# Two sets of weight sums on GpSimd, moved from two turns of the attention loop to its last turn

## The chip, the cores and the metric

The kernel runs on one core of one Trainium2 chip. A core has five engines with instruction streams of their own: TensorE (PE, with its weight loads listed as PEld), VectorE (DVE), ScalarE (ACT), GpSimd (POOL) and SyncE (SP), which here only starts transfers. The metric is the device time of one execution in microseconds (us), as a median over several runs.

## What is computed

An attention block with clusters feeds a two-layer network. Queries and keys are each assigned to the best of 16 centroids of their head; a query attends only to keys of its own cluster. The attention's output, laid out as 3072 tokens by 512 features, goes through the network with the activation h * sigmoid(1.702 h). The reference, cut to that:

```python
# q, k, v: (4 batches, 8 heads, 768, 64); centroids: (8, 16, 64); w_in (512, 2048), w_out (2048, 512)
mask = q_assign[:, :, :, None] == k_assign[:, :, None, :]
scores = np.where(mask, scale * np.matmul(q, k.transpose(0, 1, 3, 2)), -1000000000.0)
attn = np.exp(scores - np.max(scores, axis=-1, keepdims=True))
attn = attn / (np.sum(attn, axis=-1, keepdims=True) + 1e-09)
x = np.matmul(attn, v)                     # then (B,H,S,D) -> (B*S, H*D)
h = x @ w_in
g = h * (1.0 / (1.0 + np.exp(-1.702 * h)))
return g @ w_out
```

The two weight matrices arrive in double precision and are rounded on the chip.

## The kernel before

**Attention.** Heads go in pairs: 4 batches with 4 pairs each make 16 pairs (numbered 0 to 15 in the code, one to sixteen in words). A pair is done in two halves of 384 queries; a half has six units, one for each 128 keys. The main loop runs over turns `t` of two units each, so a half is three turns, a pair six, and all of attention 96 turns (`NT`), with two more to drain. The first turn of pair thirteen is turn 72, and that of pair fourteen is turn 78. The order of every engine's work is the order in which the program issues it; no scheduler moves it (`manual_schedule`). Each engine works through its own queue in order and waits at an instruction until what it needs is there.

In one turn, TensorE makes two units of transposed scores (`scores`, L453) and adds the cluster terms that push other clusters' scores far down (`part`, L476); ACT takes the exponentials into a tile `A` of 128 keys by 2 heads by 384 queries (`exps`, L484); and TensorE multiplies the previous turn's `A` with the values (`values`, L518). The softmax denominators need the sum of a half's six `A` tiles. `add_up` makes it, on GpSimd (L502, one instruction per head), except the first addition of every even half, which is VectorE's (L495), and the last two tiles of the very last half, which go to TensorE as they are (`last`). There are four `A` tiles, so an exponential can start only when GpSimd and TensorE are through with the tile of four units earlier. Once a half is summed, `row_sums_of` (L535) multiplies the sum with a constant tile on TensorE, and `normalise` (L545 to L561) turns, inverts and applies the result on VectorE. For the last batch the normalised tile goes out to memory (`kept`, L561, on SP's queue) and comes back later.

Beside that, each pair's turns prepare the next pair: its turned copies (L308, VectorE), its cluster scores (`prep_near`, L329, TensorE, once in a pair and in its first turn), its assignment and the transfers that spread it. Two of a pair's turns each also round one piece of the weights (five instructions on VectorE, two checks on ACT).

**The network.** It starts when attention ends. Both matrix products are done with seven block products in place of eight: the blocks of one operand are first added and subtracted with one another, and so are the results. For the first product, `w_in` is taken in eight strips (`f`), used for each of the four batches (`b`). For every strip a set of sums of four blocks of `w_in` is made on GpSimd, by `sums_w(i)` with i = 8 b + f. A set has four sums of 128x256 (L589 is the line of the helper that makes all such sums): S3, written in place into `w_in` and made only for the first batch, then S2, S1 and S4 in a tile `W`. There are two `W` tiles, so a set can be begun in a tile only when TensorE is through with the set two before it.

```python
        if i < FB:
            sums(nc.gpsimd, ((S[3], A11, "-", S[3]),))
        sums(nc.gpsimd, ((S[2], A22, "-", S[3]), (S[1], S[2], "+", A11),
                         (S[4], A12, "-", S[2])))
```

`first7(b, f)` makes the seven products of a strip (L743). In their order they use A11 of `w_in` (no sum), S2, S1, S3, S4, and then two more blocks of `w_in` itself. ACT copies the first result into a buffer `G` (L752), and VectorE adds the others to it (L734). After each `first7` the main loop asks for the set two ahead, `sums_w(b * FB + f + 2)`, and, for the first batch, for sums of blocks of `w_out` (`sums_z`). The sets 0 and 1 have no such place: they are made in the attention loop, at turns 72 and 78 (`NT - 24`, `NT - 18`).

Of the kernel before, what the change touches and what calls it, by code (L numbers as in the profile page):

```python
# [18 lines left out]
def kernel(  # L19
    tc: tile.TileContext,  # L20
    q: bass.AP,
    k: bass.AP,
    v: bass.AP,
    centroids: bass.AP,
    moe_w_in: bass.AP,
    moe_w_out: bass.AP,
    out: bass.AP,
):

    args = (q, k, v, centroids, moe_w_in, moe_w_out, out)
    bad = fast(tc, *args)
    with tc.If(bad > 0):
        general(tc, *args)
# [3 lines left out]
def fast(  # L39
# [172 lines left out]
    def step():  # L212

        if not now and w_done[0] < NW:
            now.append(rounding())
        if now:
            n = w_done[0]
            next(now[0])
            if w_done[0] > n:
                now.clear()  # L220
# [225 lines left out]
    def scores(u):  # L446
        g, kt = divmod(u, NJ)
        p, h = split(g)
        ps = ps_s.tile([P, 2, 512], FP32, name="s")
        for a in range(2):  # L450
            rows = slice(a * D, (a + 1) * D)
            for c in range(0, P, D):
                nc.tensor.matmul(  # L453
                    out=ps[c:c + D, a, 0:HALF],
                    lhsT=T[p, 1][rows, kt * P + c:kt * P + c + D],
                    rhs=T[p, 0][rows, h * HALF:(h + 1) * HALF],
                    start=True, stop=False)
        s_of[u] = ps[:, :, 0:HALF]

    def part(u):  # L460

        g, kt = divmod(u, NJ)
        p, h = split(g)
        if p == 0:
            for a in range(2):
                r = SQ * a
                nc.tensor.matmul(
                    out=s_of[u][:, a, :],
                    lhsT=hots[1][r:r + NC, kt * P:(kt + 1) * P],
                    rhs=hots[0][r:r + NC, h * HALF:(h + 1) * HALF],  # L470
                    start=False, stop=True)
            return
        for a in range(2):
            rows = slice(a * D, (a + 1) * D)
            for c in range(0, P, D):
                nc.tensor.matmul(  # L476
                    out=s_of[u][c:c + D, a, :],
                    lhsT=rows_of[1, p % 2][rows, kt * P + c:kt * P + c + D],
                    rhs=rows_of[0, p % 2][rows, h * HALF:(h + 1) * HALF],
                    start=False, stop=True)  # L480

    def exps(u):
        A_of[u] = ap.tile([P, 2, HALF], FP32, name="A")
        nc.scalar.activation(out=A_of[u], in_=s_of.pop(u), func=AF.Exp,  # L484
                             scale=SCALE)

    def add_up(u):

        g, kt = divmod(u, NJ)
        if kt == 0:  # L490
            return
        if kt == 1:
            sum_of[g] = ap.tile([P, 2, HALF], FP32, name="sum", bufs=2)
        if kt == 1 and g % 2 == 0:
            later.append(lambda: nc.vector.tensor_tensor(  # L495
                out=sum_of[g], in0=A_of[u - 1], in1=A_of[u], op=ALU.add))
            return
        if g == NG - 1 and kt >= NJ - 2:
            last.append(A_of[u])
            return  # L500
        for a in range(2):
            nc.gpsimd.tensor_tensor(  # L502
                out=sum_of[g][:, a],
                in0=(A_of[u - 1] if kt == 1 else sum_of[g])[:, a],
                in1=A_of[u][:, a], op=ALU.add)
# [3 lines left out]
    def values(u):  # L509
        g, kt = divmod(u, NJ)  # L510
        p, h = split(g)
        if kt == 0:
            o_of[g] = ps_o.tile([P, 2, 512], FP32, name="o")
        A = A_of.pop(u)
        for r in range(2):
            rows = slice(r * D, (r + 1) * D)
            for a in range(2):
                nc.tensor.matmul(out=o_of[g][a * D:(a + 1) * D, r, 0:HALF],  # L518
                                 lhsT=v_in[p][rows, a, kt, :],
                                 rhs=A[rows, a, :],  # L520
                                 start=(kt == 0), stop=(kt == NJ - 1))
        if kt == NJ - 1:
            o = o_of.pop(g)
            O_of[g] = (xp if p < NPAIR - HP else xl).tile(
                [P, HALF], FP32, name="x"), short()
            for r in range(2):
                nc.scalar.copy(O_of[g][r], o[:, r, 0:HALF])

    def row_sums_of(g):

        ps = ps_of[g] = bank()
        parts = (last if g == NG - 1 else []) + [sum_of.pop(g)]
        for i, sm in enumerate(parts):
            for a in range(2):
                nc.tensor.matmul(out=ps[a * D:(a + 1) * D, 0:HALF], lhsT=twos,  # L535
                                 rhs=sm[:, a, :], start=(i == 0),
                                 stop=(i == len(parts) - 1))
# [28 lines left out]
    def check(g):  # L566


        rec = recs.pop(g)
        nc.scalar.activation(out=rec, in_=rec, func=AF.Copy,  # L570
                             accum_out=row_sums[:, 0, g:g + 1])
        nc.scalar.activation(out=rec, in_=rec, func=AF.Relu, bias=top[:, 0:1],
                             scale=-2.0 * LIMIT * LIMIT,
                             accum_out=row_sums[:, 1, g:g + 1])
# [12 lines left out]
    def sums(engine, todo):  # L587
        for o, a, op, b in todo:
            engine.tensor_tensor(out=o, in0=a, in1=b, op=(  # L589
                ALU.add if op == "+" else ALU.subtract))  # L590
# [3 lines left out]
    def A_in(row, col, f):  # L594

        at = (row * FB + f) * P
        return w_in[:, 2 * col:2 * col + 2, at:at + P]
# [3 lines left out]
    def sums_w(i):  # L601

        if i >= B * FB:
            return
        f = i % FB
        S = wq.tile([P, 3, 2, P], FP32, name="W")
        w_of[i] = {1: S[:, 0], 2: S[:, 1], 3: A_in(1, 0, f), 4: S[:, 2]}
        S = w_of[i]
        A11, A12, A22 = A_in(0, 0, f), A_in(0, 1, f), A_in(1, 1, f)
# [4 lines that stand above are left out]
# [19 lines left out]
    NT = NU // 2  # L633
# [3 lines left out]
    for p in range(1, NPAIR):  # L637
        for i in range(2 if p == 1 else 0, len(PREP)):
            t = 2 * TG * (p - 1) + (0, 0, 0, 0, 1, 2, 2)[i]
# [5 lines left out]
    def prep(p, i):  # L645
        if i == 2 and p:
            load_v(p)
        PREP[i](p)
        if i in (1, 3) and loads:
            load_qk(*loads.popleft())  # L650
# [7 lines left out]
    for t in range(NT + 2):  # L658
        us = range(2 * t, 2 * t + 2) if t < NT else ()
        for u in us:  # L660
            scores(u)
        if t == 0:
            prep(0, 6)
        for u in us:
            part(u)
        for u in us:
            exps(u)
        if recs:
            check(*recs)
        for u in us:  # L670
            add_up(u)
        work = sorted(prep_at.get(t, ()), key=lambda w: PREP[w[1]] != prep_near)
        turns = [w for w in work if w[1] < 4]
        for p, i in turns:
            prep(p, i)
        work = [w for w in work if w[1] >= 4]
        while later:
            later.pop()()
        if 1 <= t <= NT:
            for u in range(2 * t - 2, 2 * t):  # L680
                values(u)
        if t >= 2 and (t - 2) % TG == TG - 1:
            row_sums_of((t - 2) // TG)
        while work and PREP[work[0][1]] == prep_near:
            prep(*work.pop(0))
        if t in (NT - 24, NT - 18):
            sums_w(t // (NT - 18))
        if t >= NT - 8 and t < NT:
            XT = next(made)
        for p, i in work:  # L690
            prep(p, i)
        for _ in range(0 if t in (0, 1, 2, NT - 1) else 5 if t == 4 else
                       steps[t % (2 * TG)]):
            step()
        if t >= 2 and (t - 2) % TG == TG - 1:
            normalise((t - 2) // TG)
# [607 lines left out]
```

## Time and profile before

| | |
|---|---|
| median of 3 runs | 939.36 us (939.26 to 939.95) |
| profiled execution, its time | 939.74 us |
| profiled execution, its span | 937.8 us |
| PE busy | 920.5 us (98% of the span) |
| PEld busy | 578.4 us (62%) |
| VectorE busy | 624.0 us (67%) |
| ACT busy | 326.0 us (35%) |
| GpSimd busy | 420.8 us (45%), of which 266.2 us additions of A tiles at L502 (252, mean 1091 ns) |
| first product of the network (L743) | starts at 352.95 us |
| granted TensorE clock | 0.997 of full speed |

Times inside the profile count from the span's start. A line of the order in time gives the start, the busy time of the run of instructions, engine, line, operation, the tile written and read, the shape, the count, and in brackets how long the engine had been idle and who released it. The share of busy time is a mean over two parts that differ: attention up to 352.95 us, and the network after it, so the prediction reads stretches, not the whole.

### The profile page before, as it was taken

To read this page: it belongs to the slowest core of one execution; us is meant where nothing else is said; L and a number is where in the kernel's file an instruction comes from. 1 tells how busy PE (TensorE), PEld (TensorE's weight loads), DVE (VectorE), ACT (ScalarE), POOL (GpSimd) and SP (SyncE) were. 2 spreads that over 40 slices of the span, in tenths; PEclk is the share of its full clock that TensorE was granted. 3 is DMA by queue.
4 is the path that set the end of the run, shared out by engine and by line. 5 is a ranking of instruction groups with operands and counts; after the bars stand their busy time and mean duration, and the time that the engine had idled before them with its cause. 6 is when DMAs were issued, how large, how long until landed. Compare 5 with 4: busy or idle time off the path is not lost.

```text
span 937.8 us, 16591 instructions
## 1 busy us (share of the span) xinstructions
PE 920.5 (98%) x6469; PEld 578.4 (62%) x6469; DVE 624.0 (67%) x1077; ACT 326.0 (35%) x703; POOL 420.8 (45%) x440
## 2 busy tenths in 40 slices
PE   6999999999999999999999999999999999999997
PEld 2344444444444445558886557887557887556886
DVE  3999999989988896775345775344776343677331
ACT  3667767767776672221001221001222000232000
POOL 5899899899999996772001220001211000120000
PEclk9999999999999999999999999999999999999999
DMA  9465556566543210011000000000000000000000
GB/s 184 101 128 101 99 103 138 106 121 114 103 99 98 81 49 10 0 29 40 23 23 22 1 0 1 23 23 24 0 1 1 23 23 23 0 1 1 23 24 26
DMA packets 138215, 46.65 MB, mean 50 GB/s; under 512 B 127256, under 2 KB 132496, under 8 KB 138128
## 3 DMA queue, kind: packets, MB, share of 16 engines
q1 hardware_dynamic: 137984, 45.48, 22.1%
q8 instruction: 53, 0.87, 0.4%
q14 instruction: 34, 0.28, 0.1%
q10 hardware_dynamic: 144, 0.03, 0.0%
HBM read 37.44 MB, written 8.05 MB: 49 GB/s over the span
## 4 chain that ended last, share of the span: by engine, by line
PE 84%; POOL 4%; DVE 4%; issue 3%; ACT 2%; DMA 1%; SPq 1%; ACTq 0%; DVEq 0%; POOLq 0%
PE b L800 31%; PE b L743 31%; PE s L453 9%; PE o L518 7%; POOL sum L502 4%; PE m L535 2%; PE s L476 2%; ACT A L484 1%; PE m L329 1%; DMA line<-row 0%; DVE x L556 0%; SPq L404 0%; DMA raw<-in_moe_w_out_dram 0%; DVE e L200 0%; PE m L315 0%
## 5 line engine op out<-in xcount | busy, mean ns | idle before, releaser
L502 POOL TENSOR_TENSOR sum<-sum,A 128x384 f32<-128x384 f32 x252 | 266.2, 1091 | 33.6 <-ACT A L484 21.3
L589 POOL TENSOR_TENSOR W<-w_in 128x256 f32<-128x256 f32 x32 | 23.3, 729 | 379.6 <-PE b L743 379.4
L484 ACT ACTIVATE A<-s 128x768 f32<-128x768 f32 x192 | 145.1, 804 | 99.4 <-PE s L476 76.3
L734 DVE TENSOR_TENSOR G<-b,G 128x384 f32<-128x384 f32 x224 | 124.4, 556 | 62.7 <-PE b L743 50.4
L453 PE MATMUL s<-T,T 64*64 64x384 f32 x1536 | 145.8, 494 | 2.7 <-ACT A L484 0.7
L734 DVE TENSOR_TENSOR y<-b,y 128x256 f32<-128x256 f32 x72 | 29.5, 423 | 171.7 <-PE b L800 121.8
L518 PE MATMUL o<-A,inv 64*64 64x384 f32 x1536 | 141.5, 483 | 0.0
L579 ACT ACTIVATE th<-G 128x384 f32<-128x384 f32 x128 | 67.0, 523 | 208.8 <-DVE G L734 128.5
L580 DVE SCALAR_TENSOR_TENSOR G<-th,G 128x384 f32<-128x384 f32 x128 | 91.3, 713 | 23.0 <-ACT th L579 19.1
L453 PEld LDWEIGHTS s<-T,T 64*64 64x64 f32 x1536 | 52.7, 132 | 79.0 <-ACT A L484 51.3
L743 PE MATMUL b<-x,W 128*128 128x384 f32 x256 | 93.0, 486 | 0.0
L743 PE MATMUL b<-T,w_in 128*128 128x384 f32 x256 | 93.0, 486 | 0.0
L743 PE MATMUL b<-x,w_in 128*128 128x384 f32 x256 | 88.5, 486 | 0.0
L800 PE MATMUL b<-Z,G 128*128 128x256 f32 x384 | 86.8, 379 | 0.0
L800 PE MATMUL b<-w_out,G 128*128 128x256 f32 x384 | 84.8, 379 | 0.0
L518 PEld LDWEIGHTS o<-A,inv 64*64 64x64 f32 x1536 | 58.9, 133 | 38.3 <-issue 33.2
L800 PEld LDWEIGHTS b<-w_out,G 128*128 128x128 f32 x384 | 72.8, 190 | 10.9
L800 PEld LDWEIGHTS b<-Z,G 128*128 128x128 f32 x384 | 73.0, 190 | 9.9
L743 PEld LDWEIGHTS b<-x,W 128*128 128x128 f32 x256 | 48.6, 190 | 33.9
L743 PEld LDWEIGHTS b<-T,w_in 128*128 128x128 f32 x256 | 48.6, 190 | 33.9
L743 PEld LDWEIGHTS b<-x,w_in 128*128 128x128 f32 x256 | 48.6, 190 | 33.6 <-issue 0.6
L810 ACT COPY y<-b 128x256 f32<-128x256 f32 x12 | 4.5, 372 | 141.5 <-PE b L800 141.5
(120 smaller groups left out, 1130.6 us busy)
## 6 DMA issues: line engine op xcount, KB each, us to landing
raw<-in_moe_w_in_dram SPq DMA_DIRECT2D x16, 512.0 KB
raw<-in_moe_w_out_dram SPq DMA_DIRECT2D x16, 512.0 KB
inv<-in_v_dram SPq DMA_DIRECT2D x16, 384.0 KB
in<-in_q_dram SPq DMA_DIRECT2D x60, 96.0 KB
in<-in_k_dram SPq DMA_DIRECT2D x60, 96.0 KB
out_dram<-y SPq DMA_DIRECT2D x12, 256.0 KB
out_dram<-y SPq DMA_DIRECT2D x24, 128.0 KB
rows<-line SPq DMA_DIRECT2D x120, 1.5 KB
```

Source lines behind the costliest of these rows:

```text
L453: nc.tensor.matmul(out=ps[c:c + D, a, 0:HALF], lhsT=T[p, 1][rows, kt * P + c:kt * P + c + D], rhs=T[p, 0][rows, h * HALF:(h + 1) * HALF], ...
L476: nc.tensor.matmul(out=s_of[u][c:c + D, a, :], lhsT=rows_of[1, p % 2][rows, kt * P + c:kt * P + c + D], rhs=rows_of[0, p % 2][rows, h * HA ...
L484: nc.scalar.activation(out=A_of[u], in_=s_of.pop(u), func=AF.Exp, scale=SCALE)
L502: nc.gpsimd.tensor_tensor(out=sum_of[g][:, a], in0=(A_of[u - 1] if kt == 1 else sum_of[g])[:, a], in1=A_of[u][:, a], op=ALU.add)
L518: nc.tensor.matmul(out=o_of[g][a * D:(a + 1) * D, r, 0:HALF], lhsT=v_in[p][rows, a, kt, :], rhs=A[rows, a, :], start=(kt == 0), stop=(kt = ...
L535: nc.tensor.matmul(out=ps[a * D:(a + 1) * D, 0:HALF], lhsT=twos, rhs=sm[:, a, :], start=(i == 0), stop=(i == len(parts) - 1))
L579: nc.scalar.activation(out=t, in_=h, func=AF.Tanh, scale=1.702)
L580: nc.vector.scalar_tensor_tensor(out=g, in0=t, scalar=1.0, in1=h, op0=ALU.add, op1=ALU.mult)
L589: engine.tensor_tensor(out=o, in0=a, in1=b, op=(ALU.add if op == "+" else ALU.subtract))
L734: nc.vector.tensor_tensor(out=o, in0=p, in1=a, op=ALU.add)
L743: nc.tensor.matmul(out=ps[:, 0:HALF], lhsT=a[:, c], rhs=x(c), start=(c == 0), stop=(c == 1))
L800: nc.tensor.matmul(out=ps[:, 0:DN], lhsT=a(f // 4)[:, f % 4], rhs=z(f), start=(f == 0), stop=(f == FB - 1))
```

## The change

The two calls leave turns 72 and 78, where they stood behind the values, the row sums and `prep_near`. Both now stand in the last turn, turn 95, directly behind its `add_up`. In that turn `add_up` issues nothing to GpSimd, since the last two tiles go to TensorE; so in GpSimd's queue the eight sums come right behind the last additions of turn 94 and in front of set 2, and no other queue is touched. The waits on them change with their place: TensorE's products with S2, S1 and S4 of sets 0 and 1 now wait on GpSimd, as those of all other sets do.

```diff
         for u in us:
             add_up(u)
+        if t == NT - 1:
+            sums_w(0)
+            sums_w(1)
         work = sorted(prep_at.get(t, ()), key=lambda w: PREP[w[1]] != prep_near)
...
         while work and PREP[work[0][1]] == prep_near:
             prep(*work.pop(0))
-        if t in (NT - 24, NT - 18):
-            sums_w(t // (NT - 18))
         if t >= NT - 8 and t < NT:
             XT = next(made)
```

## The prediction

> **What bounds the kernel now.** I read the page first, then the busy time of each engine in stretches cut at one repeated event, then the waits of those stretches, then the order in time on GpSimd and on TensorE at the end of attention. On the page, the 40 slices of the busy part:
>
> ```profile
> PE   6999999999999999999999999999999999999997
> ...
> POOL 5899899899999996772001220001211000120000
> ```
>
> Each digit is a tenth of 23.4 us. TensorE is full from start to end; GpSimd (POOL) is nearly full in the first 15 slices, which are attention, and mostly idle after them. So there are two candidates for the limit in attention, and shares cannot tell them apart. For that I cut attention at the moment when TensorE makes the cluster scores of the next pair (L329, once in each pair of heads, six turns). It starts at 229.60, 250.16, 270.71, 292.98 and 315.55 us; the last two rows end where the same place in the turn is reached without it (336.11) and at the first product of the MoE part (352.95). Columns: the stretch and its length, then busy us (and instructions) of PE, weight loads, DVE, ACT, POOL, then clock and DMA.
>
> ```profile
> 229.60:250.16 20.56, 20.42 (x267) 9.27 (x265) 18.49 (x31) 14.51 (x32) 18.60 (x19) 1.00 0.54 112
> 250.16:270.71 20.55, 20.42 (x267) 9.27 (x265) 18.49 (x31) 14.49 (x32) 19.45 (x20) 1.00 0.54 111
> 270.71:292.98 22.27, 21.95 (x267) 9.64 (x265) 18.52 (x31) 14.71 (x32) 22.11 (x23) 1.00 0.56 115
> 292.98:315.55 22.57, 22.12 (x265) 9.58 (x264) 18.86 (x31) 14.81 (x32) 22.49 (x22) 1.00 0.37 103
> 315.55:336.11 20.56, 20.42 (x265) 9.27 (x265) 19.62 (x33) 14.60 (x33) 18.63 (x19) 1.00 0.14 48
> 336.11:352.95 16.84, 16.75 (x194) 7.37 (x192) 13.84 (x20) 10.38 (x24) 16.68 (x15) 1.00 0.07 24
> ```
>
> The reader should see that a pair takes 20.56 us, with TensorE 20.42 of them, and that this repeats in the stretch after as in those before. GpSimd has about 2.0 us to spare there. In two stretches it is otherwise: GpSimd is full (22.11 of 22.27, 22.49 of 22.57) and the pair is longer. Those hold the two sets of sums at L589. The set of turn 72 starts at 268.81 and is felt in the stretch after that mark, the set of turn 78 lies just ahead of 292.98 and is felt after it. GpSimd in order of time (start, duration, and the tile written):
>
> ```profile
> 268.81 1.44 POOL L589 TENSOR_TENSOR w_in<-w_in 128x256 f32<-128x256 f32 x1
> ...
> 292.10 0.72 POOL L589 TENSOR_TENSOR w_in<-w_in 128x256 f32<-128x256 f32 x1
> 292.90 0.73 POOL L589 TENSOR_TENSOR W<-w_in 128x256 f32<-128x256 f32 x1
> 293.71 0.73 POOL L589 TENSOR_TENSOR W<-W,w_in 128x256 f32<-128x256 f32 x1
> 294.39 0.73 POOL L589 TENSOR_TENSOR W<-w_in,W 128x256 f32<-128x256 f32 x1
> 295.08 1.33 POOL L502 TENSOR_TENSOR sum<-sum,A 128x384 f32<-128x384 f32 x1
> ```
>
> From start to start, the first set takes 268.81 to 272.50, 3.69 us, and the second 292.10 to 295.08, 2.98 us. Who is held up by it, from the waits of 270.71 to 315.55 (total us, times, longest):
>
> ```profile
> ACT A L484 <- POOL sum L502: 3.9, 4, 1.5
> PEld m L535 <- POOL sum L502: 3.6, 5, 0.9
> ```
>
> The exponentials need a free A tile (four of them), which GpSimd gives back by adding it up; the row sums on TensorE need the finished sum. In 229.60 to 270.71 the same two waits are 1.7 and 1.2 us. So two pairs are bound by GpSimd, all others by TensorE.
>
> **What the skill says.** The Trainium skill, GPSIMD Engine Reference, section Specifications, says that GpSimd shares its SBUF interfaces with VectorE and meets contention with VectorE instructions that have two SBUF inputs. The trace agrees: the first sum of the set at 268.81 took 1.44 us, beside VectorE's addition of two A tiles (L495, 268.44 to 269.65), where the same form took 0.72 at 292.10. Perfetto Trace Analysis, section GPSIMD Engine Instruction, advises timing GpSimd by the spacing of starts; I do so. Trainium Architecture — The Big Picture, section Inside one NeuronCore, has engines synchronise only through semaphores, so a wait exists only where the program has one. In the order of the changed program, TensorE's first product of the MoE part has none on GpSimd; the second waits for the count of the second sum of set 0, the third for the third, the fifth for the fourth. The row sums of the last half pair wait for the last additions alone, the same two as before.
>
> **Part removed.** Eight sums leave turns 72 and 78. Taken as GpSimd time they are 3.69 + 2.98 = 6.67 us. As time on the path they are only what the two pairs lost against TensorE's pace: 22.27 - 20.555 = 1.72 and 22.57 - 20.555 = 2.02 (20.555 is the mean of the two stretches before). The sum is 3.73 us. What is late next is TensorE itself at 20.56 a pair, which cannot be undercut by taking work from GpSimd. The third pair (315.55 to 336.11) already runs at 20.56, although it starts with GpSimd behind and with the DMA of the kept tiles; so the other novelties of these last pairs cost nothing and I expect the two pairs at 20.56. From there to the MoE part everything moves earlier as a block: GpSimd's last run of additions begins after a wait for ACT of 0.96 us at 335.76, so no backlog reaches into it.
>
> **Part added.** The eight sums now follow GpSimd's last addition, in front of set 2, whose first operation stands there already:
>
> ```profile
> 347.59 4.52 POOL L502 TENSOR_TENSOR sum<-sum,A 128x384 f32<-128x384 f32 x4
> 352.06 0.73 POOL L589 TENSOR_TENSOR w_in<-w_in 128x256 f32<-128x256 f32 x1
> ...
> 352.16 0.19 PEld L535 LDWEIGHTS m<-sum,twos 128*64 128x64 f32 x2 [0.32 <-POOL sum L502]
> 352.95 0.94 PEld L743 LDWEIGHTS b<-x,w_in 128*128 128x128 f32 x4 [0.60 <-issue]
> 354.02 1.16 PEld L743 LDWEIGHTS b<-T,W 128*128 128x128 f32 x4
> 355.31 1.16 PEld L743 LDWEIGHTS b<-x,W 128*128 128x128 f32 x4
> ```
>
> I keep the times of before; all move by 3.73. GpSimd is free at 352.06 (its last addition reaches TensorE at 352.16). With the spacing of the set at 292.10 (0.80, 0.81, 0.68, 0.69), the second sum of set 0 is done by 353.67, when the third, which waits for it, would start; TensorE loads its weights at 354.02. Slack 0.35 us, cost nothing. The third is done by 354.35 against 355.31, the fourth by 355.04 against 357.89. Set 1 begins at 355.04 and has its second sum at 356.65; TensorE wants it at 363.06, slack 6.4. Set 2's first sum moves from 352.06 to 358.02, and its second waits in both kernels for TensorE until 359.82. Behind it nothing changes. No transfer is issued or moved by the sums; SP's queue keeps its order.
>
> Beside the sums, VectorE normalises the last half pair. Its transposes (353.06 to 354.53) have one input; its addition at 354.44 has two in SBUF, took 0.53 in this place and 1.07 beside the sums at 294.47. So VectorE ends about 0.54 later, and so do the transfer of the kept tile (issued at 355.59) and ACT's first copy into G (358.01, 0.48 long), which waits for it. TensorE needs that copy for its seventh product, at 360.48: slack 1.99 us becomes 1.45. Cost nothing.
>
> What this trace does not show is the first sum with VectorE idle but at this place, after four crowded additions. Low bound: no wait. High bound: the spacing of 1.51 us seen at 268.81; then the second sum is done at 354.38 and TensorE waits 0.36, and if the second were stretched likewise, about 0.7. I take no wait, since VectorE stands idle from 350.3 to 353.06; 0.7 stays for the range.
>
> **The sum.** 939.74 us for the profiled execution (span 937.8 and 1.94 around it) less 3.73 gives 936.0. The median of the three runs, 939.36, is 0.38 lower; on that footing 935.6, which I forecast, 0.4% less.
>
> **Rivals.**
> - The wait at the handover gives part back: 0.36 to 0.7 us on TensorE's second product, 936.0 to 936.3. For it: slack is only 0.35. Against: VectorE is idle then. Chance 0.12.
> - All of GpSimd's 6.67 us come off: 932.7. For it: GpSimd is full in both pairs. Against: TensorE's 20.42 of 20.56 in the neighbours. Chance 0.03.
> - Nothing comes: the two pairs are long for another reason (the first kept tiles go out there, and SP's loads behind them), 939.4. Against: the third pair has them too and takes 20.56. Chance 0.03.
> - Slower: TensorE's first product is held until both sets are done, with every sum stretched to the longest third sum of the trace, 1.08 us: 352.06 + 8 x 1.08 + 0.1 = 360.8 against 352.95, a wait of 7.9, net +4.1, 943.5. It decides once the wait passes 3.73 us and shows as slower from 5.6. For it: GpSimd works in order and both sets stand ahead. Against: the waits named above are by single sums. Chance 0.02.
>
> The forecast has 0.80. A difference under 0.2% (1.9 us) cannot be told from none; so faster is 0.80 + 0.12 + 0.03 = 0.95, rounded down to 0.94, no change 0.04, slower 0.02. The range takes the forecast with 0.7 us of scatter below (the three runs span 0.69) and, above, 0.7 for the handover and 0.5 for scatter: 934.9 to 936.8.
>
> **What would show it.** Right: the two stretches between cluster scores at 20.5 to 20.6 us and the first product of the MoE part near 349.2; the waits of ACT and TensorE on GpSimd back to the size of other pairs; eight L589 sums in a row behind the last addition; no idle of TensorE in front of its second and third product; the MoE part 584 us as now. Wrong: a stretch of more than 21 us there, or weight loads of the second product waiting for GpSimd.

## The result, and the profile after

The changed kernel takes 936.0 us (median of 6 runs, 934.95 to 936.74) against 939.57 us for the kernel before (6 runs, 939.24 to 939.95): a ratio of 0.9959, with a 95% interval of 0.9949 to 0.997. That is 3.6 us less, clear of no change and inside the range of the prediction. The profiled execution of after is the slowest of its six, 936.74 us, with a span of 934.8 us, so its span is only 3.0 us shorter. Where the two numbers differ is shown below.

The busy time of after in the same stretches, cut at the cluster scores of L329; the last two rows end as before at the same place of the turn without them and at the network's first product. Columns as in the prediction: stretch, length, busy us of PE, weight loads, DVE, ACT, POOL, clock, DMA.

```profile
230.15:250.72 20.57, 20.42 (x267) 9.28 (x265) 18.48 (x31) 14.51 (x32) 18.59 (x19) 1.00 0.56 112
250.72:271.28 20.56, 20.42 (x267) 9.27 (x265) 18.49 (x31) 14.52 (x32) 18.57 (x19) 1.00 0.53 112
271.28:291.83 20.55, 20.55 (x266) 9.61 (x264) 18.50 (x31) 14.52 (x32) 18.55 (x19) 1.00 0.58 118
291.83:312.38 20.55, 20.41 (x266) 9.27 (x264) 18.51 (x31) 14.50 (x32) 18.58 (x19) 1.00 0.47 119
312.38:332.94 20.56, 20.41 (x266) 9.27 (x264) 19.58 (x33) 14.63 (x32) 18.59 (x19) 1.00 0.15 48
332.94:349.85 16.91, 16.83 (x195) 7.42 (x193) 13.90 (x21) 10.37 (x24) 16.83 (x16) 1.00 0.06 24
```

The two long pairs are gone (a pair, as before, is the work on two heads, six turns). From the cluster scores of turn 66 to the last place, before took 336.11 - 250.16 = 85.95 us and after takes 332.94 - 250.72 = 82.22: 3.73 us less, all of it in the third and fourth rows. GpSimd is back at 18.6 us in each of them. In the waits of after from 271.28 to 312.38, GpSimd holds up the other engines for

```profile
ACT A L484 <- POOL sum L502: 1.7, 2, 0.8
PEld m L535 <- POOL sum L502: 1.2, 2, 0.6
```

which is what two undisturbed pairs, pairs without a set in them, had before. At the handover, where attention ends and the network's first product starts, GpSimd in order of time, and below it TensorE's weight loads for the first five products:

```profile
344.49 4.51 POOL L502 TENSOR_TENSOR sum<-sum,A 128x384 f32<-128x384 f32 x4
348.97 0.72 POOL L589 TENSOR_TENSOR w_in<-w_in 128x256 f32<-128x256 f32 x1
349.77 0.73 POOL L589 TENSOR_TENSOR W<-w_in 128x256 f32<-128x256 f32 x1
350.57 0.73 POOL L589 TENSOR_TENSOR W<-W,w_in 128x256 f32<-128x256 f32 x1
351.26 0.73 POOL L589 TENSOR_TENSOR W<-w_in,W 128x256 f32<-128x256 f32 x1
351.94 1.04 POOL L589 TENSOR_TENSOR w_in<-w_in 128x256 f32<-128x256 f32 x1
```

```profile
349.85 0.94 PEld L744 LDWEIGHTS b<-x,w_in 128*128 128x128 f32 x4 [0.60 <-issue]
350.92 1.16 PEld L744 LDWEIGHTS b<-T,W 128*128 128x128 f32 x4
352.21 1.16 PEld L744 LDWEIGHTS b<-x,W 128*128 128x128 f32 x4
353.50 1.16 PEld L744 LDWEIGHTS b<-T,w_in 128*128 128x128 f32 x4
354.79 1.16 PEld L744 LDWEIGHTS b<-x,W 128*128 128x128 f32 x4
```

No load behind the first has a bracket: TensorE waits for none of the sums. The third sum, which itself waits for the second, starts at 350.57; the load that needs the second comes at 350.92.

That the span shrank by 3.0 and not 3.7 us was settled for the most part in the first 25 us, where the change has no part. The same columns for 15 to 24 us, first before, then after:

```profile
15.00:18.00 3.00, 1.36 (x14) 0.57 (x15) 1.61 (x3) 2.21 (x3) 0.00 (x0) 0.89 1.22 201
18.00:21.00 3.00, 3.00 (x24) 0.72 (x20) 0.96 (x1) 0.34 (x2) 0.00 (x0) 0.54 1.31 206
21.00:24.00 3.00, 3.00 (x44) 1.34 (x48) 0.69 (x2) 1.28 (x2) 2.28 (x3) 1.00 1.06 152
```

```profile
15.00:18.00 3.00, 1.77 (x12) 0.68 (x16) 1.32 (x3) 2.10 (x3) 0.00 (x0) 0.61 1.19 186
18.00:21.00 3.00, 3.00 (x20) 0.68 (x16) 0.68 (x1) 0.64 (x1) 0.00 (x0) 0.50 1.20 221
21.00:24.00 3.00, 3.00 (x36) 1.12 (x32) 0.12 (x1) 0.87 (x2) 2.70 (x3) 0.75 1.10 164
```

The third number from the end, 0.89, 0.54, 1.00 against 0.61, 0.50, 0.75, is TensorE's granted clock. If low means half, as the 0.50 suggests, it was low for 3.4 us in before and for 6.8 us in after (estimates from these means), and the first cluster scores came at 22.96 us instead of 22.35. The account of the span: 3.73 gained in the pairs; 0.56 lost at the start (250.72 against 250.16 at the same mark), 0.07 in the last stretch (16.91 against 16.84), 0.10 from the network's first product to the end (584.95 against 584.85). Together 3.0.

### The profile page after: what moved, and what is told of

It is laid out like the page before. It is cut to its first block, busy times and chain, and to the rows that moved or that the text cites. A ratio compares the mean times of both kernels' runs of the same rounds, so it can differ in the third digit from the quotient of the medians.

```text
span 934.8 us, 16594 instructions
## 1 busy us (share of the span) xinstructions
PE 918.1 (98%) x6469; PEld 578.4 (62%) x6469; DVE 623.5 (67%) x1077; ACT 325.5 (35%) x703; POOL 418.5 (45%) x440
## 4 chain that ended last, share of the span: by engine, by line
PE 90%; DVE 4%; ACT 2%; issue 1%; DMA 1%; SPq 1%; POOL 0%; ACTq 0%; DVEq 0%
PE b L801 31%; PE b L744 31%; PE s L453 12%; PE o L518 9%; PE s L476 3%; PE m L535 2%; ACT A L484 1%; PE m L329 1%; DMA line<-row 0%; DVE x L556 0%; SPq L404 0%; DMA raw<-in_moe_w_out_dram 0%; DVE e L200 0%; PE m L315 0%; DVE m L193 0%
## 5 line engine op out<-in xcount | busy, mean ns | idle before, releaser
L502 POOL TENSOR_TENSOR sum<-sum,A 128x384 f32<-128x384 f32 x252 | 264.0, 1083 | 39.0 <-ACT A L484 24.8
L589 POOL TENSOR_TENSOR W<-w_in 128x256 f32<-128x256 f32 x32 | 23.4, 730 | 373.3 <-PE b L744 373.1
```

The lines of the kernel that those rows point to most:

```text
L502: nc.gpsimd.tensor_tensor(out=sum_of[g][:, a], in0=(A_of[u - 1] if kt == 1 else sum_of[g])[:, a], in1=A_of[u][:, a], op=ALU.add)
L589: engine.tensor_tensor(out=o, in0=a, in1=b, op=(ALU.add if op == "+" else ALU.subtract))
```

## The experiments

The theory to test: a pair is as long as TensorE's 20.56 us unless GpSimd needs longer, for which it has 1.96 us to spare (20.56 less its 18.60), and behind the last addition the sums cost nothing. Medians of before in the two series were 939.77 (29 runs) and 939.74 (33 runs).

**One set moved, one left.** Set 0 in the last turn, set 1 in turn 78.

```diff
         if t == NT - 1:
             sums_w(0)
-            sums_w(1)
...
+        if t == NT - 18:
+            sums_w(1)
```

> Set 0 is made in the last turn, set 1 still in turn 78. Theory (a pair is as long as the slower of TensorE, 20.56 us, and GpSimd): the stretch from turn 72's cluster scores on falls from 22.27 to 20.56, and the one that holds set 1 stays longer by what the set has over GpSimd's spare time, 2.98 - 1.96 = 1.0, up to the 2.02 that it cost before: 21.6 to 22.6. Median 937.0 to 938.0. Rival, every us of GpSimd counts: only 3.69 of 6.67 comes off, the stretch is 23.5, median about 939.0. Rival, the pairs were long for another reason than the sums: no stretch differs from after, 936.0.

Measured: 937.54 us (12 runs, 936.7 to 938.39), ratio to before 0.9975 (0.9967 to 0.9984). Its stretches around set 1:

```profile
271.16:291.71 20.55, 20.55 (x266) 9.62 (x264) 18.51 (x31) 14.51 (x32) 19.46 (x20) 1.00 0.56 118
291.71:313.99 22.28, 21.96 (x267) 9.64 (x265) 18.52 (x31) 14.73 (x32) 22.20 (x22) 1.00 0.43 110
```

The pair without a set is at 20.55, the one with it at 22.28. The set takes 3.69 us of GpSimd here, not 2.98 (its first sum starts at 289.82, beside VectorE's addition, and the next addition at 293.51), and 3.69 less 1.96 to spare is the loss of 1.72, the same as set 0 caused at turn 72 in the kernel before. Set 1 in the kernel before doesn't fit this sum: it took 2.98 and cost 2.02, not 1.0, with GpSimd already late from set 0. The pair is long where a set is and not where it was taken away: the sums are the cause of the long pairs, and a us of GpSimd in a pair is not a us of the kernel.

**No sums for the two sets.** The products read blocks of `w_in` instead, so two of the eight strips are not the network's (in every batch, since S3 is made once for all four).

```diff
         if t == NT - 1:
-            sums_w(0)
-            sums_w(1)
+            for i in range(2):
+                w_of[i] = {1: A_in(0, 0, i), 2: A_in(0, 0, i),
+                           3: A_in(1, 0, i), 4: A_in(0, 0, i)}
```

> The sums of sets 0 and 1 are left out altogether (the first products of two strips read blocks of w_in as they are, so the output of those strips is not the network's). Theory (the handover is free): the stretch from the last cluster-score place to the network's first product, and the first products after it, stay within 0.15 us of after; median 936.0 +- 0.5. Rival, the sums at the handover cost TensorE 0.4 to 0.7 us: faster by that, and the network's first strip shorter by that.

Measured: 935.99 us (5 runs, 935.15 to 936.57), ratio 0.9961 (0.9947 to 0.9974), the same as after. The last stretch of attention:

```profile
332.52:349.39 16.87, 16.79 (x194) 7.38 (x192) 13.87 (x20) 10.38 (x24) 16.79 (x16) 1.00 0.07 24
```

It is 0.04 us shorter than after's 16.91, and from the first product to the ninth both take 10.4 us (349.39 to 359.82, and 349.85 to 360.27 in after). There is nothing left to gain from the eight sums.

**The sets in reverse order.**

```diff
         if t == NT - 1:
-            sums_w(0)
             sums_w(1)
+            sums_w(0)
```

> In the last turn set 1 is made ahead of set 0. Theory (TensorE's second product waits for the second sum of set 0 alone): that sum is done 2.97 + 1.61 = 4.6 us after GpSimd's last addition instead of 1.6, TensorE wants it at 1.95: a wait of 2.6 us, nothing behind it, median 938.6. Rival, TensorE has room there (the products' waits are taken up later, as the network has slack): 936.0. Rival, the first product is held until both sets are done: no change from after either, and after itself would show the wait.

Measured: 939.0 us (13 runs, 937.94 to 941.17), ratio 0.9995 (0.9987 to 1.0003): most of the gain is gone, and the rest cannot be told from none. TensorE at the handover, and GpSimd with set 0:

```profile
349.43 1.56 PE L744 MATMUL b<-x,w_in 128*128 128x384 f32 x4
353.40 1.56 PE L744 MATMUL b<-T,W 128*128 128x384 f32 x4 [2.42 <-POOL W L589]
354.79 1.45 PE L744 MATMUL b<-x,W 128*128 128x384 f32 x4
```

```profile
351.50 1.04 POOL L589 TENSOR_TENSOR w_in<-w_in 128x256 f32<-128x256 f32 x1
352.62 0.72 POOL L589 TENSOR_TENSOR W<-w_in 128x256 f32<-128x256 f32 x1
353.42 0.72 POOL L589 TENSOR_TENSOR W<-W,w_in 128x256 f32<-128x256 f32 x1
```

The first product starts on time, the second 3.97 us after it instead of 1.39: a loss of 2.58, against 2.6 expected, and the third follows at 1.39. TensorE starts at 353.40, when the second sum of set 0 is ready. So that one sum is what it waits for, and a wait there is lost in full. A further 0.2 us of this profile is one pair of 20.78 us without a sum in it, in which TensorE waited 0.32 us for a transfer of the assignment (`rows`, L476).

**Two sums in each of four pairs.** The eight sums go, two at a time, into turns 54, 60, 66 and 72, and no pair has more than two. With `few`, `sums_w` hands back its list of four sums instead of issuing them.

```diff
-        if t == NT - 1:
-            sums_w(0)
-            sums_w(1)
...
+        if t in (NT - 42, NT - 36, NT - 30, NT - 24):
+            if t in (NT - 42, NT - 30):
+                todo = sums_w(0 if t == NT - 42 else 1, few=True)
+            sums(nc.gpsimd, todo[:2])
+            todo = todo[2:]
```

> The eight sums are made two at a time in the first turns of pairs ten to thirteen (turns 54, 60, 66, 72), about 1.5 to 2.2 us for each pair. Theory (GpSimd has 1.96 us to spare in a pair and loses nothing to TensorE until that is used up): all four stretches 20.56 to 20.8, median 936.0 to 936.8. Rival, every us of GpSimd counts: 6.0 to 6.7 us more than after, 942 to 943, as before or slower. Rival, GpSimd's spare time is not usable, since it lies in waits that the sums do not fill: each stretch longer by about 0.9, median about 939.6, as before.

Measured: 937.28 us (10 runs, 936.78 to 937.91), ratio 0.9975 (0.9966 to 0.9985): between the theory and its rivals. The four stretches:

```profile
209.13:229.71 20.58, 20.42 (x267) 9.28 (x265) 19.02 (x31) 14.58 (x32) 20.58 (x21) 1.00 0.49 106
229.71:250.91 21.20, 21.05 (x267) 9.45 (x265) 17.98 (x31) 14.63 (x32) 21.12 (x22) 1.00 0.58 117
250.91:271.47 20.56, 20.41 (x265) 9.27 (x264) 18.76 (x31) 14.64 (x32) 20.56 (x20) 1.00 0.47 101
271.47:292.99 21.52, 21.42 (x266) 9.81 (x265) 18.61 (x31) 14.63 (x32) 21.52 (x21) 1.00 0.59 125
```

They lose 0.02, 0.64, 0 and 0.96, 1.6 in all. GpSimd is full in every one (20.58 of 20.58, and so on) although two sums take 1.5 to 2.2 us and it had 2.0 to spare. The missing time is in its additions at L502: eighteen of them, the work of a pair, take 18.6 us without waits in an undisturbed pair, and 18.9, 19.6, 18.9 and 19.6 in these. The theory that GpSimd has a fixed 1.96 us to spare falls here.

Where that time goes can be read at single additions. First an undisturbed pair of after, then the second pair of this run:

```profile
240.27 1.00 POOL L502 TENSOR_TENSOR sum<-sum,A 128x384 f32<-128x384 f32 x1 [0.83 <-ACT A L484]
248.46 1.20 DVE L495 TENSOR_TENSOR sum<-A 128x768 f32<-128x768 f32 x1
249.80 1.00 POOL L502 TENSOR_TENSOR sum<-sum,A 128x384 f32<-128x384 f32 x1 [0.96 <-DVE sum L495]
```

```profile
238.29 0.73 DVE L200 SCALAR_TENSOR_TENSOR e<-raw,e 128x512 f32<-128x512 uint32 x1
238.38 1.50 POOL L502 TENSOR_TENSOR sum<-A 128x384 f32<-128x384 f32 x1
248.00 1.21 DVE L495 TENSOR_TENSOR sum<-A 128x768 f32<-128x768 f32 x1
248.36 1.70 POOL L502 TENSOR_TENSOR sum<-sum,A 128x384 f32<-128x384 f32 x1
```

The spare time is mostly two waits, one for an exponential and one for VectorE's addition of two A tiles. When GpSimd is late it no longer waits there. It works on beside VectorE, and the addition takes 1.50 or 1.70 us instead of 1.00. In the nine traces, between 30 and 340 us, 1246 additions lie beside none of VectorE's instructions that read two tiles from SBUF (L200, L495, L556, L589), and each takes 0.95 to 1.01 us, counted to the next start less the wait before it; every addition of more than 1.1 us lies beside one of them.

**The same, two turns later in the pair.** Turns 56, 62, 68 and 74, away from VectorE's addition of two A tiles; the diff is the one above with 40, 34, 28 and 22 in place of 42, 36, 30 and 24.

> As e4_spread, two sums in each of pairs ten to thirteen, but two turns later in the pair (turns 56, 62, 68, 74), where VectorE does not add two A tiles. Theory (in e4_spread the two sums took 2.1 to 2.2 us beside that addition, more than the 1.7 us that 18.87 us of additions leave in 20.56; here they take 1.5): all four stretches 20.5 to 20.7, median 936.0 to 936.5. Rival, the sums' time beside VectorE does not matter and a full GpSimd queue costs by itself: 0.4 us a pair again, median 937.3.

Measured: 938.25 us (21 runs, 937.54 to 939.17), ratio 0.9985 (0.9978 to 0.9992). Neither came: it is slower than both, by about 1 us against the earlier turns. Two of its four pairs stayed at 20.57 us; the other two:

```profile
229.54:251.51 21.97, 21.27 (x266) 9.45 (x264) 19.31 (x31) 14.63 (x33) 21.85 (x21) 1.00 0.56 117
251.51:273.09 21.58, 21.27 (x265) 9.45 (x264) 18.78 (x31) 14.61 (x33) 21.05 (x21) 1.00 0.49 105
```

The sums themselves were short (0.72 to 0.74 us each), and the eighteen additions of each of these pairs took 19.6 us, as in the longer pairs of the spread sums above. In the first of them GpSimd needs less than in the second pair above, 20.97 us (229.66 to 250.63) against 21.74 (228.29 to 250.03), and yet the pair is longer, 21.97 against 21.20. So the length of GpSimd's work does not explain why these turns do worse; that stays open.

**Five A tiles in the kernel before.** Sets in turns 72 and 78 as before.

```diff
-    ap = att.enter_context(tc.tile_pool(name="ap", bufs=4))
+    ap = att.enter_context(tc.tile_pool(name="ap", bufs=5))
```

> The kernel before, sets in turns 72 and 78, with five A tiles instead of four. Theory (GpSimd's backlog reaches TensorE by two ways, a free A tile for the exponentials and the finished sum for the row sums; with one way widened the other takes over): 938.5 to 939.8, the waits of the row sums on GpSimd grow where those of the exponentials go. Rival, the A tiles alone pass it on: the two stretches fall to 20.6 to 21.2 us and the median to 936.0 to 937.5, without any move of the sums.

Measured: 939.48 us (13 runs, 939.09 to 939.84), ratio 1.0001 (0.9993 to 1.0009). The waits on GpSimd from 270.46 to 315.31, the two pairs with the sets:

```profile
PEld m L535 <- POOL sum L502: 3.6, 5, 0.8
...
PE m L535 <- POOL sum L502: 0.5, 3, 0.2
```

The 3.9 us of waits of the exponentials are gone altogether, and the kernel is no faster: the two stretches are 22.28 and 22.57. It was expected that the waits of the row sums grow in their place; they did not (3.6 us before and now). So the row sums, which wait for the finished sum in TensorE's own queue, are enough to pass on GpSimd's lateness, and the waits for A tiles, listed first in the profile of before, added nothing to it.

**Both sets ahead of the last additions.**

```diff
+        if t == NT - 2:
+            sums_w(0)
+            sums_w(1)
         for u in us:
             add_up(u)
-        if t == NT - 1:
-            sums_w(0)
-            sums_w(1)
```

> Both sets stand in turn 94, ahead of GpSimd's last four additions instead of behind them. Theory (the last row sums wait for the last addition, and nothing covers the sums there): the row sums of the last half pair and with them the network's first product come later by the time of the eight sums, 6.0 to 6.7 us; median 942.0 to 942.7, slower than before. Rival, GpSimd has room before the last additions (its share in that stretch is busy time that could be waiting): 936 to 938.

Measured: 943.42 us (4 runs, 942.69 to 944.53), ratio 1.004 (1.0025 to 1.0056), slower than before. TensorE there:

```profile
346.94 1.51 PE L535 MATMUL m<-A,twos 128*64 128x384 f32 x8
353.53 2.49 PE L535 MATMUL m<-sum,twos 128*64 128x384 f32 x4 [5.08 <-POOL sum L502]
355.95 2.93 PE L744 MATMUL b<-x,w_in 128*128 128x384 f32 x4
358.67 1.97 PE L744 MATMUL b<-T,W 128*128 128x384 f32 x4
360.47 1.45 PE L744 MATMUL b<-x,W 128*128 128x384 f32 x4
```

From the last place without cluster scores (332.68) to the first product it is 23.27 us instead of 16.91: 6.36 more. That the size is the expected one is luck in part. The eight sums take 6.39 us; the four additions behind them take 0.68 less than in after (3.80 instead of 4.48); and from the last wait of the row sums to the first product it is 0.68 more (1.47 instead of 0.79), at a lower clock. The median lies 0.7 us above the range that was expected. The first two products there are slow, and TensorE's clock fits that, the same columns as above:

```profile
350.00:352.00 2.00, 0.00 (x0) 0.00 (x0) 0.00 (x0) 0.00 (x0) 2.00 (x3) 1.00 0.00 0
352.00:354.00 2.00, 0.47 (x1) 0.29 (x2) 0.00 (x0) 0.00 (x0) 2.00 (x3) 0.72 0.00 0
354.00:356.00 2.00, 2.00 (x5) 0.34 (x3) 0.00 (x0) 0.00 (x0) 1.10 (x2) 0.50 0.00 0
...
358.00:360.00 2.00, 2.00 (x5) 1.18 (x4) 0.55 (x1) 0.30 (x2) 0.00 (x0) 0.58 0.26 98
```

Behind the wait of 5.08 us the granted clock is 0.5, and the first product takes 2.72 us to the next start instead of 1.39.

No version of these beats after, and none is in sight in this place: without the sums the time is the same, and TensorE is busy for 20.4 of a pair's 20.56 us.

## Why the prediction was right

- **What bounds what.** TensorE at 20.56 us a pair, but GpSimd in the two pairs with sets. After shows both pairs at 20.55, and one set left behind brings back 1.72.
- **The part removed, 3.73 us.** Measured 3.73 in the same stretches. The step that mattered was to price the sums by what two pairs lost against their neighbours and not by the 6.67 us of GpSimd. The rival that takes all 6.67 is out: TensorE's pace stayed.
- **Which wait passes it on.** The prediction named two, free A tiles and row sums. The second alone is enough, as five A tiles showed. The sum did not depend on this.
- **The handover.** Slack of 0.35 us for the second sum: 0.35 measured (350.57 to 350.92). The named high bound of 0.7 was not needed. Leaving the sums out gains 0.04 us in the last stretch, and reversing the sets loses 2.58: the wait exists, and in this order the slack covers it.
- **VectorE beside the sums.** Its addition took 1.06 us instead of 0.53, forecast 1.07, and ACT's first copy came 5.59 us after the first product instead of 5.06, forecast 0.54 later. TensorE had room for it. (The copy ended at 355.92; the seventh product's weights were loaded at 357.37, a slack of 1.45 as forecast.) Not foreseen: the same meeting stretched the first sum of set 1 to 1.04 us, in a slack of 6.4.
- **The rival on the slower side** put the wait on the first product. That one waits for nothing on GpSimd, as the prediction read from the order of the program; the reversed sets show that it starts on time. A slower kernel of this kind exists, though, with the sums in front of the last additions.
- **The size.** 935.6 forecast, 936.0 measured. Half of the difference is the starting point: the forecast took 3.73 from a median of 939.36 over three runs, and six runs give 939.57. From there the gain is 3.57, and the 0.16 that is missing lies inside the scatter of the runs (934.95 to 936.74).
- **What the prediction took too simply**, without harm: that GpSimd has "about 2.0 us to spare" in a pair. The spread sums showed that this is not a store to draw on: it is two waits, and beside one of them stands an addition of VectorE that stretches GpSimd's own. The forecast did not use it: it took the loss from the measured lengths of the pairs.

## What to carry to other kernels

Price work that is taken off a crowded engine by what its stretch lost against undisturbed neighbours, not by its own time; here 3.7 of 6.7 us. When the work has to go somewhere, look for the place behind that engine's last item on the path and check the first consumer by name and by slack: 0.35 us were enough, and the order of two equal blocks was worth 2.6. Time to spare that a profile shows between an engine's instructions need not be usable: ask what the neighbours do in it. Two attempts to fill it lost 1.6 and 2.4 us in their pairs, against nothing for the same work at the end.

## What the runs showed of the hardware

TensorE's granted clock fell to 0.5 in a wait of 5.08 us and stayed low for about 6.8 us (an estimate from the 0.72, 0.50 and 0.58 above: from about 352.9 to 359.7); in the wait of 2.42 us in the run with reversed sets, and behind it, it stayed at 1.00. The Trainium skill, TensorE: Matmul & The Clock Gate, section Part 1: The HAM clock gate, gives about 3.4 us of idling as the window after which the clock is halved; both runs agree with it. It makes a long wait dearer than its length: there, the two products behind it took 1.8 us more than at full clock (2.72 and 1.80 us instead of 1.39 and 1.29).

GpSimd's additions of 128x384 are not of fixed length: 0.95 to 1.01 us with no two-input instruction of VectorE beside them, up to 1.35 beside L556, 1.51 beside L200 and 1.69 beside L495. The Trainium skill, GPSIMD Engine Reference, section Specifications, names the contention with VectorE's instructions that have two SBUF inputs, and these traces agree. It meets both sides: a sum of 128x256 took 1.04 to 1.45 us beside VectorE's additions and 0.72 without, and VectorE's addition at L556 took 1.06 beside a sum and 0.53 without.
